# Moving the first transfers, one strip's weight stream and the start of attention in a hand-ordered attention and MLP kernel

## The chip, the cores and the metric

The kernel runs on one core of a Trainium2 chip. The metric is the device time of one execution in microseconds (us); the median of several runs stands for the kernel. All data are fp32, apart from the raw weights, which arrive as fp64 and are converted by the kernel.

## The reference

```python
def _attn_ref(q, k, v, g_norm):                    # (8, 8, 576, 64) each
    kv = np.einsum('bhsd,bhse->bhde', k, v)
    out = np.einsum('bhsd,bhde->bhse', q, kv)
    rms = np.sqrt(np.mean(out * out, axis=-1, keepdims=True) + 1e-06)
    return (out / rms * g_norm).astype(np.float32)

def _moe_ref(x, w_in, w_out):                      # 4608 tokens, 512 -> 2048 -> 512
    h = x @ w_in
    r = np.maximum(h, 0.0)
    g = r * r
    return (g @ w_out).astype(np.float32)

# x is the attention's output, transposed to (batch * seq, heads * dim)
```

Linear attention without a softmax: each head's 64 x 64 matrix kv is built first, and each query row is multiplied by it, divided by its root mean square and scaled. The result feeds a two-layer MLP with a squared relu.

## The kernel before

**Strips.** The 4608 tokens are worked on in nine strips of 512, numbered 0 to 8 in the program. In a strip, "up" is the product with w_in and the squared relu, "down" is the product with w_out and the output. Both use Strassen's scheme: seven products of sums of blocks in place of eight products of blocks. Strip 0 has a plain up (`first_up`, `up_first`) and a down of seven products, in the order 1, 2, 5, 6, 7, 3, 4, each in two halves (`down`, L729 in `product`). Strip 1 has an up of seven products and a down in which the scheme is used twice (`down_deep`, L944). Strips 2 to 8 use it twice in both; their up consists of 55 slots (`up_slot`, L1132 the matmuls, L1144 the sums behind them). The sums of blocks are elementwise work: of weights, of x, of the activations (tiles gt, g_s) and of results (snap, o_sb). Most of it runs on VectorE (DVE), through the helper `minus` (L287) and others; some on GpSimd (POOL). ScalarE (ACT) evacuates results and does the squared relus.

**Attention.** Heads go in pairs p of 0 to 3. `transposed_query` (T) transposes q (on TensorE, L399, for the first batches), `key_value` (K, L427) builds kv, `first_queries` (Q, L541) or `query` multiplies, and the mean of squares (L480), root and reciprocal with Newton steps (L481 to L495, one of them on ACT at L486) lead to x_n (L548 in strip 0, L531 later). x_n is transposed again on TensorE (xt_ps, L565 and L591) or written to memory and read back (x_q, x_d) in late strips. `first_normalized` (N) and `first_features` (F) are these steps of the first strip. All these steps are entries of one list, `slices`, in the order in which they are to be issued; `attend(n)` issues them up to entry n, and the loop over a strip's steps calls it between matmul steps.

**The weights at the start.** The raw w_in and w_out come in pieces of 512 KB (`load_piece`, L237). A piece is first read by ACT (`convert_on_act`, L249 and L252) and then converted by four DVE instructions (`conversion`, L261, L263, L267, L270); `first_piece` issues a number of these steps, so that (piece, (0, 4)) is all four of piece 0. `load_more` keeps loads ahead. `first_up` (U, L576) uses the converted pieces. `keep_busy(ps, n)` (L371) issues n matmuls with the identity whose result is not used.

**The weight stream.** `stream(n)` issues the loads of the next n blocks of w_out (or of sums of w_in) into tiles w_blk of the pool `stream_pool`, which has four buffers of 1 MB (L824 for the blocks of strip 0). The same pool gives `reserve(p)` its tile w_t: for the second use of the scheme, sums of the weight block of product p are made on DVE (`deep_sums`, L287) and stored to memory (`store_deep_sums`, L857; product 6 has its own small tiles, L851). `down` puts product p in `deep_due` at its first half (product 1 at its second), and the loop over strip 0's steps takes it from there. A tile of a pool waits for its buffer's last use: of a w_blk that is the last matmul with it, of a w_t the landing of its store. `store_first(b)` stores three block combinations that were made in SBUF.

**Order and queues.** The program sets the order of every engine's instructions by hand (`manual_schedule`). Each engine runs its instructions in that order, and an instruction waits for its inputs and for its buffers. Nearly all loads and stores are issued on SyncE's queue (SP) in program order; each carries one of eight semaphores in turn.

In strip 0 the steps are numbered i; the first `n_up` are the up part. What follows a step of the down part there:

```python
            if i == n_up:
                stream()
            if i == n_up + 3:
                store_first(2)
...
            while deep_due and i != n_up + 1:
                store_deep_sums(*deep_due.popleft())
```

Of the kernel before, what the change touches and what calls it, by code (L numbers as in the profile page):

```python
# [10 lines left out]
FP32 = mybir.dt.float32  # L11
# [9 lines left out]
def kernel(  # L21
# [34 lines left out]
    nc = tc.nc  # L56
    P = 128
# [4 lines left out]
    NP = H // 2  # L62
    FC = d_ff // P
    C = S // P
# [33 lines left out]
    ctx.enter_context(tc.manual_schedule())  # L98


    main = {}

    def load(b, p, q_eng, names="kvq", parts=range(4)):
        hs = slice(2 * p, 2 * p + 2)
        inputs = (("q", q, q_eng), ("k", k, nc.sync), ("v", v, nc.sync))
        if b == 0 and p >= 2:

            h_place = g_pool.tile([P, 4, C * P], FP32, name="first_qkv", tag="gt")
        if b == 1 and p == 2:
            h_place = spare_pool.tile([P, 3, C * P], FP32, name="more_qkv")  # L110
        placed = (b, p) in ((0, 2), (0, 3), (1, 2))
        for i, (n, src, eng) in enumerate(inputs if b == 0 else inputs[1:] + inputs[:1]):
            if n not in names:
                continue
            whole = src[b, hs, 0 : C * P].rearrange("h (sp c) d -> sp h c d", c=C)
            if n == "q" and b >= Q_ON_PE:

                t = qkv_pool.tile([P, 4 * C, SQ], FP32, name=n, tag=n, bufs=3) if 0 in parts else main[n, b, p]
                for a in parts:
                    h, f = divmod(a * SQ, D)  # L120
                    eng.dma_start(
                        out=t[ts(a, SQ)],
                        in_=src[b, 2 * p + h, 0 : C * P, f : f + SQ].rearrange("(k i) f -> i k f", k=4 * C),
                    )
            elif n != "q":
                if placed:
                    t = h_place[:, i].rearrange("p (h c d) -> p h c d", h=2, c=C)
                else:
                    t = qkv_pool.tile([P, 2, C, D], FP32, name=n, tag=n)
                eng.dma_start(out=t, in_=whole)  # L130
            elif b == 0:

                if placed:
                    t = h_place[:, i].rearrange("p (h c d) -> p h c d", h=2, c=C)
                else:
                    t = qkv_pool.tile([P, 2, C, D], FP32, name=n, tag=n, bufs=3)
                eng.dma_start(out=t, in_=whole)
            else:

                if placed:  # L140
                    t = h_place[:, i].rearrange("p (c h d) -> p c h d", h=2, c=C)
                else:
                    t = qkv_pool.tile([P, C, 2, D], FP32, name=n, tag=n, bufs=3)
                for h in range(2):
                    eng.dma_start(out=t[:, :, h, :], in_=whole[:, h])
            main[n, b, p] = t
# [34 lines left out]
    def load_next(q_eng=nc.sync, names="kvq"):  # L181
        u = next(to_load, None)
        if u is not None:
            load(*u, q_eng, names)
# [49 lines left out]
    def load_piece():  # L234
        if len(raw) < len(sources):
            t = raw_pool.tile([P, 2, WN // 2], I64, name="raw", tag="raw")
            nc.sync.dma_start(out=t, in_=sources[len(raw)])  # L237
            raw.append(t)
# [42 lines left out]
    def load_more(end):  # L281

        while len(raw) < min(end + 8, max(len(sources) - 4, end + 4), len(sources)):
            load_piece()
# [60 lines left out]

    load_next()
    load_rest(0, nc.sync)
    for p in range(1, NP):
        load_next()
        load_piece()  # L350
    load_more(0)
    g_col = const.tile([P, 1], FP32, name="g_col")
    g_src = g_norm.rearrange("(d u) -> d u", u=1)
# [13 lines left out]
    def keep_busy(ps, n):  # L367


        for _ in range(n):  # L370
            nc.tensor.matmul(ps, lhsT=ident, rhs=ident[:, : ps.shape[1]], start=True, stop=True)  # L371
# [38 lines left out]
    def key_value(b, *ps_of):  # L410
        while any(f == load and a[:2] == (b, p) or f == load_rest and a[0] == b for _, f, a in keys_due for p in ps_of):
            _, f, a = keys_due.popleft()
            f(*a)
        ps = apsum.tile([P, len(ps_of), D], FP32, name="kv_ps", tag="at")
        if (b, ps_of[0]) == (0, 0):
            keep_busy(ps[:, 0], 5)
            warm = apsum.tile([P, NT, P], FP32, name="x_ps", tag="first")[:, 0]
        half = slice(REST * (b % 2), REST * (b % 2 + 1))
        tiles = [[main.pop((n, b, p)) for n in "kv"] for p in ps_of]
        steps = [(i, c) for i in range(len(ps_of)) for c in range(C)] + [(i, C) for i in range(len(ps_of))]  # L420
        for i, c in steps:
            if (b, ps_of[i], c) == (0, 0, C):
                keep_busy(warm, 2)
            for h in range(2):
                at = (slice(None), h, c) if c < C else (half, 2 * ps_of[i] + h)
                a, w = (t[at] for t in (tiles[i] if c < C else (k_rest, v_rest)))
                nc.tensor.matmul(  # L427
                    ps[ts(h, D), i], lhsT=a, rhs=w, start=i == 0 and c == 0, stop=c == C, skip_group_check=True
                )
        at = (NP * b + ps_of[0]) % (2 * NP)  # L430
        d = kv_all[:, at : at + len(ps_of)]
        nc.scalar.copy(d[0:D, :, 0:D], ps[0:D])
        nc.scalar.copy(d[D:P, :, D:P], ps[D:P])
        for i, p in enumerate(ps_of):
            kvd[b, p] = d[:, i]
            if b < 2:
                if b == 1 and p == 0:
                    load_next()
            else:
                u = next(to_load, None)  # L440
                if u is not None:
                    keys_later(load, *u, nc.sync, "kv")
                if p == NP - 1 and b + 1 < B:
                    keys_later(load_rest, b + 1, nc.sync)
# [192 lines left out]
        convert_on_act, transposed_query, key_value, first_queries, first_normalized, first_features, first_piece  # L637
    )
    U = first_up
    slices += [(T, (0, 0)), (K, (0, 0)), (T, (0, 1)), (Q, (0,)), (K, (0, 1)), (N, (0,)), (act, (0,)), (piece, (0, 4))]  # L640
    slices += [(T, (0, 2)), (Q, (1,)), (F, (0,)), (K, (0, 2)), (N, (1,)), (act, (1,)), (U, (0, [0])), (piece, (1, 4))]
    slices += [(T, (0, 3)), (Q, (2,)), (F, (1,)), (U, (0, [1])), (K, (0, 3)), (N, (2,)), (act, (2,))]
    slices += [(Q, (3,)), (U, (0, [2])), (F, (2,)), (U, (1, [0])), (piece, (2, 1)), (N, (3,)), (act, (3,))]
    slices += [(piece, (2, 3)), (U, (1, [1, 2])), (F, (3,)), (piece, (3, 4))]
    slices += [(U, (2, [0, 1, 2])), (U, (3, [0, 1, 2]))]
    ready[0] = len(slices)
# [212 lines left out]
    def down(s, p, i):  # L859
        if i == 0:  # L860
            open_bank(p)
        a = {1: 11, 2: 21, 6: 11, 7: 12, 3: 21, 4: 22}.get(p)
        w = w_blk[s, p]
        product(
            p, i,
            lambda fc: (gq[s, 1, fc // 2][:, fc % 2] if p == 5 else gq[s, a][:, fc])[:, ts(i, P)],
            lambda fc: w[:, :, fc], FQ,
        )

        if i == (p == 1) and s == DEEP - 1:  # L870
            deep_due.append((p, w))
        if i == 0:
            return
        del w_blk[s, p]

        if s == 0 and p in (2, 6, 3):
            reserve({2: 5, 6: 7, 3: 4}[p])
        if p not in (1, 7) and (s, p) not in ((0, 3), (0, 4)):
            stream()
        if p == (1 if s else 2):  # L880
            for g in range(NG):
                x = gq[s, 11][:, ts(g, 2)]
                minus(nc.vector, x, gq[s, 1, g], x)
        if p == (2 if s else 6):
            minus(nc.vector, gq[s, 21], gq[s, 21], gq[s, 11])

        def store(th, eh):
            def f(b, a=None):
                o = out_tile()
                if a is None:  # L890
                    nc.scalar.copy(o, b)
                else:
                    nc.vector.tensor_tensor(out=o, in0=b, in1=a, op=ALU.add)
                send(s, th, eh, o)
            return f

        combine(p, store(0, 0), store(0, 1), store(1, 0), store(1, 1))
# [284 lines left out]
    for s in range(N_STRIP):  # L1182
# [23 lines left out]
        for i, (w, fn, a) in enumerate(steps):  # L1206
# [33 lines left out]
            if s:  # L1240
# [6 lines left out]
                elif not due(keys_due) and not (soon and due(tiles_due)):  # L1247
                    least = 2.1 if s == DEEP else 4.5 if i < n_up else 3.3
                    quiet = n_up * 2 // 3 < i < n_up + 3 or s == DEEP and i > n_up + 5
                    if not quiet and clock[0] >= dripped[0] + least:  # L1250
                        dripped[0] = clock[0]
                        drip(True)
                pace = 25 if s == DEEP else 36
                attend(begun + (goal - begun) * min(i + 1, pace) // pace)
                if s == DEEP and i == n_up - 3:
                    leaf_sums(s, 4)
                if s == 1 and i in range(2, 23, 3):
# [2 lines left out]
                    stream()  # L1260
                continue
            if i == n_up:
                stream()
            if i == n_up + 3:
                store_first(2)
            if i in (n_up + 8, n_up + 11):
# [8 lines left out]
            n = i + 1 - (n_up - 6)  # L1275
            pairs, m = divmod(max(n - 2 * NP, 0), 3)
            attend(min(ready[0] + min(max(n, 0), 2 * NP) + (n >= 2 * NP) + 4 * pairs + (0, 2, 2)[m], goal))
            while deep_due and i != n_up + 1:
                store_deep_sums(*deep_due.popleft())
            if 11 <= i < n_up:  # L1280

# [31 lines left out]
```

## Time and profile before

| what | value |
|---|---|
| median of 3 runs | 898.0 us (897.18 to 898.66) |
| profiled execution | 897.15 us |
| its span, from the first to the last instruction | 895.1 us |
| granted TensorE clock, mean | 1.00 |
| busy: PE (TensorE matmul) | 880.4 us, 98% |
| busy: DVE (VectorE) | 734.5 us, 82% |
| busy: ACT (ScalarE), POOL (GpSimd) | 315.7 us, 307.1 us |
| moved by DMA | 235.71 MB, 263 GB/s |

Busy times are those of a profiled execution on the core; a span of 895.1 us holds 20697 instructions. "PE" is the matmul side of TensorE, "PEld" its weight loads, which overlap; "SPq" is SyncE's queue of DMA issues. L12 is line 12 of the kernel. A group "out<-in" names the tiles that an instruction writes and reads. Two records of an fp32 matmul with a 128x128 block of moving data start about 0.112 us apart, so an extra distance between starts is time in which TensorE waited.

### The profile page before, as it was taken

The numbers are of one execution on the slowest core, as the hardware profiler recorded it, in microseconds if no ns is written. First come the engines' busy times: TensorE is split into PE (matmuls) and PEld (weight loads), VectorE is DVE, ScalarE is ACT, GpSimd is POOL, SyncE is SP. The second block draws the span as 40 slices with busy tenths as digits, with TensorE's granted clock in tenths as the row PEclk, the third lists the DMA queues.
The fourth block names the chain that finished last, engine by engine and source line by source line (L and its number), as shares of the span: only waits on it lengthen the run. The fifth ranks groups of instructions, "written<-read, shape, count | busy, mean of one in ns | idle before, by whom it ended". The sixth has DMA issues, their size and how long they took to land.

```text
span 895.1 us, 20697 instructions
## 1 busy us (share of the span) xinstructions
PE 880.4 (98%) x8300; PEld 823.0 (92%) x8300; DVE 734.5 (82%) x1256; ACT 315.7 (35%) x622; POOL 307.1 (34%) x315
## 2 busy tenths in 40 slices
PE   8999999999999999999999999999999999999998
PEld 7445878889999999999999999999999999999998
DVE  3999999779779986898689966895899779875886
ACT  4798241320027302640255023801271027102710
POOL 0000005700558233632373035604460447044700
PEclk9999999999999999999999999999999999999999
DMA  9998998999988798969877989798748865884384
GB/s 303 307 316 250 310 330 267 289 314 323 313 197 279 266 326 238 277 249 317 250 232 238 323 239 248 237 297 292 218 143 297 304 203 164 301 299 154 128 316 180
DMA packets 169231, 235.71 MB, mean 263 GB/s; under 512 B 79408, under 2 KB 134192, under 8 KB 160688
## 3 DMA queue, kind: packets, MB, share of 16 engines
q1 hardware_dynamic: 168976, 234.40, 81.2%
q8 instruction: 65, 1.06, 0.5%
q14 instruction: 30, 0.25, 0.1%
q10 hardware_dynamic: 160, 0.00, 0.0%
HBM read 197.66 MB, written 36.70 MB: 262 GB/s over the span
## 4 chain that ended last, share of the span: by engine, by line
PE 74%; DVE 13%; DMA 6%; issue 2%; ACT 2%; SPq 2%; DVEq 0%; ACTq 0%
PE ps_B L944 22%; PE ps_A L944 17%; PE ps_A L1132 15%; PE ps_B L1132 8%; PE ps_A L729 4%; PE ps_C L1132 3%; PE ps_B L729 2%; PE kv_ps L427 1%; DVE w_c L267 1%; PE x_ps L463 1%; DVE gt L1144 1%; DMA w_blk<-w_in_deep 1%; DVE w_t L287 1%; DMA v_rest<-in_v_dram 1%; DMA x_d<-x_q 1%
## 5 line engine op out<-in xcount | busy, mean ns | idle before, releaser
L944 PE MATMUL ps_B<-w_blk,g_s 128*128 128x128 f32 x1024 | 126.2, 275 | 0.0
L944 PEld LDWEIGHTS ps_B<-w_blk,g_s 128*128 128x128 f32 x1024 | 120.0, 192 | 0.2
L1132 PE MATMUL ps_A<-x_l,w_in 128*128 128x128 f32 x784 | 104.1, 276 | 0.0
L287 POOL TENSOR_TENSOR x_l<-xT 128x256 f32<-128x256 f32 x21 | 16.2, 769 | 246.4 <-PE ps_A L944 246.4
L944 PE MATMUL ps_B<-w_blk,gt 128*128 128x128 f32 x768 | 97.4, 275 | 0.0
L1132 PEld LDWEIGHTS ps_A<-x_l,w_in 128*128 128x128 f32 x784 | 95.4, 192 | 0.5 <-DVE gt L1144 0.2
L944 PE MATMUL ps_A<-w_blk,g_s 128*128 128x128 f32 x768 | 93.6, 275 | 0.0
L944 PEld LDWEIGHTS ps_B<-w_blk,gt 128*128 128x128 f32 x768 | 91.5, 192 | 0.1
L944 PEld LDWEIGHTS ps_A<-w_blk,g_s 128*128 128x128 f32 x768 | 89.6, 192 | 0.0
L1144 POOL TENSOR_TENSOR snap<-snap,gt 128x512 f32<-128x512 f32 x35 | 46.6, 1332 | 118.9 <-ACT snap L1149 54.7
L1149 ACT COPY snap<-ps_A 128x512 f32<-128x512 f32 x63 | 36.7, 583 | 133.5 <-PE ps_A L1132 119.5
L1082 ACT ACTIVATE gt<-gt 128x512 f32<-128x512 f32 x112 | 69.6, 622 | 18.1 <-DVE gt L1144 18.0
L959 DVE TENSOR_TENSOR o_sb<-o_sb,ps_B 128x256 f32<-128x256 f32 (+1 forms) x128 | 49.5, 387 | 30.9 <-ACT o_sb L960 19.2
L944 PE MATMUL ps_A<-w_blk,gt 128*128 128x128 f32 x576 | 72.3, 275 | 0.0
L1083 ACT ACTIVATE gt<-gt 128x512 f32<-128x512 f32 x112 | 70.6, 631 | 3.6
L944 PEld LDWEIGHTS ps_A<-w_blk,gt 128*128 128x128 f32 x576 | 68.2, 192 | 0.4 <-DMA w_blk<-w_deep 0.2
L1144 POOL TENSOR_TENSOR gt<-gt,snap 128x512 f32<-128x512 f32 x42 | 52.6, 1278 | 23.8 <-DVE snap L1144 23.7
L287 DVE TENSOR_TENSOR gt<-gt 128x2048 f32<-128x2048 f32 (+1 forms) x29 | 59.7, 2063 | 0.0
L1042 POOL TENSOR_TENSOR w_i<-w_in 128x512 f32<-128x512 f32 x7 | 9.7, 1382 | 142.2 <-DVE w_in L287 141.5
L960 ACT COPY o_sb<-ps_A 128x128 f32<-128x128 f32 x24 | 6.4, 266 | 146.2 <-PE ps_A L944 146.2
L1132 PE MATMUL ps_A<-x_l,w_blk 128*128 128x128 f32 x392 | 52.2, 276 | 1.3 <-issue 1.2
L1132 PE MATMUL ps_B<-x_l,w_blk 128*128 128x128 f32 x392 | 52.0, 276 | 0.0
(180 smaller groups left out, 1811.7 us busy)
## 6 DMA issues: line engine op xcount, KB each, us to landing
w_blk<-w_deep SPq DMA_DIRECT2D x56, 1024.0 KB, 6.8
w_blk<-w_out SPq DMA_DIRECT2D x56, 768.0 KB, 6.0
w_blk<-w_in_deep SPq DMA_DIRECT2D x49, 768.0 KB, 4.8
raw<-in_moe_w_in_dram SPq DMA_DIRECT2D x16, 512.0 KB, 7.4
raw<-in_moe_w_out_dram SPq DMA_DIRECT2D x16, 512.0 KB, 6.2
k<-in_k_dram SPq DMA_DIRECT2D x29, 256.0 KB, 4.8
v<-in_v_dram SPq DMA_DIRECT2D x29, 256.0 KB, 5.0
x_d<-x_q SPq DMA_DIRECT2D x27, 256.0 KB, 5.3
```

What stands on the lines that cost most here:

```text
L267: yield nc.vector.scalar_tensor_tensor(out=ci, in0=high, scalar=-(2**30), in1=ci, op0=ALU.bitwise_and, op1=ALU.bitwise_or)
L287: eng.tensor_tensor(out=out, in0=a, in1=b, op=ALU.subtract)
L427: nc.tensor.matmul(ps[ts(h, D), i], lhsT=a, rhs=w, start=i == 0 and c == 0, stop=c == C, skip_group_check=True)
L729: nc.tensor.matmul(bank[BANK[p]][:, i, :], lhsT=lhsT(k), rhs=rhs(k), start=p in (1, 5, 2) and i == 0 and k == 0, stop=k == n - 1, skip_gro ...
L944: nc.tensor.matmul(chain[c][x][:, i, :], lhsT=a[:, f, :], rhs=w[:, f, :], start=x not in opened[c] and f == 0, stop=f == FQ // 2 - 1, skip ...
L959: add = lambda out, a, b: nc.vector.tensor_tensor(out=out, in0=a, in1=b, op=ALU.add)
L1042: nc.gpsimd.tensor_tensor(out=s1, in0=w_half(b, 0, 1), in1=w_half(b, 1, 1), op=ALU.add)
L1082: nc.scalar.activation(o, o, AF.Relu)
L1083: nc.scalar.activation(o, o, AF.Square)
L1132: nc.tensor.matmul(ps[:, i, :], lhsT=w, rhs=rhs, start=j in (1, 2, 5) and i == 0, stop=True, skip_group_check=True)
L1144: add = lambda eng, out, a, b: eng.tensor_tensor(out=out, in0=a, in1=b, op=ALU.add)
L1149: nc.scalar.copy(t, ps)
```

## The change

Four places change.

- **First loads.** For pairs 2 and 3 of batch 0, q is loaded ahead of a raw piece, and k and v behind it; before, a raw piece followed each pair's q, k and v. `first_places` keeps the tile of such a pair between the two calls of `load`.
- **First warm-up and first slices.** `keep_busy` ahead of the first `key_value` issues 3 matmuls instead of 5. In the list of the opening's steps, the fourth conversion step of pieces 0 and 1 is taken apart from the first three and comes later, the first U moves behind T of pair 3, and U with index 2 of tile 0 moves ahead of the last Q.
- **Strip 0's down part.** Two blocks (6 and 7) are streamed at its first step instead of one; the loads at the end of products 5 and 6 go, and one (block 4) is issued after the first half of product 6. The sums of product 5's weights, which were made after its first half, are made after its second.
- **Attention of strips 2 and on.** The slices of the next strip are spread over steps 5 to 40 of a strip in place of 0 to 35. For strip 1 nothing changes there.

```diff
-    main = {}
+    main, first_places = {}, {}
...
         if b == 0 and p >= 2:
-
-            h_place = g_pool.tile([P, 4, C * P], FP32, name="first_qkv", tag="gt")
+            if p not in first_places:
+                first_places[p] = g_pool.tile([P, 4, C * P], FP32, name="first_qkv", tag="gt")
+            h_place = first_places[p]
...
     load_next()
     load_rest(0, nc.sync)
-    for p in range(1, NP):
-        load_next()
+    load_next()
+    for p in range(2, NP):
+        load(0, p, nc.sync, "q")
         load_piece()
+        load(0, p, nc.sync, "kv")
+        next(to_load)
     load_more(0)
...
-            keep_busy(ps[:, 0], 5)
+            keep_busy(ps[:, 0], 3)
...
-    slices += [(T, (0, 0)), (K, (0, 0)), (T, (0, 1)), (Q, (0,)), (K, (0, 1)), (N, (0,)), (act, (0,)), (piece, (0, 4))]
-    slices += [(T, (0, 2)), (Q, (1,)), (F, (0,)), (K, (0, 2)), (N, (1,)), (act, (1,)), (U, (0, [0])), (piece, (1, 4))]
-    slices += [(T, (0, 3)), (Q, (2,)), (F, (1,)), (U, (0, [1])), (K, (0, 3)), (N, (2,)), (act, (2,))]
-    slices += [(Q, (3,)), (U, (0, [2])), (F, (2,)), (U, (1, [0])), (piece, (2, 1)), (N, (3,)), (act, (3,))]
+    slices += [(T, (0, 0)), (K, (0, 0)), (T, (0, 1)), (Q, (0,)), (K, (0, 1)), (N, (0,)), (act, (0,)), (piece, (0, 3))]
+    slices += [(T, (0, 2)), (Q, (1,)), (F, (0,)), (K, (0, 2)), (piece, (0, 1)), (N, (1,)), (act, (1,)), (piece, (1, 3))]
+    slices += [(T, (0, 3)), (U, (0, [0])), (Q, (2,)), (F, (1,)), (U, (0, [1])), (K, (0, 3)), (piece, (1, 1)), (N, (2,))]
+    slices += [(act, (2,)), (U, (0, [2])), (Q, (3,)), (F, (2,)), (U, (1, [0])), (piece, (2, 1)), (N, (3,)), (act, (3,))]
...
-        if p not in (1, 7) and (s, p) not in ((0, 3), (0, 4)):
+        if p not in (1, 7) and (s, p) not in ((0, 5), (0, 6), (0, 3), (0, 4)):
             stream()
...
-                pace = 25 if s == DEEP else 36
-                attend(begun + (goal - begun) * min(i + 1, pace) // pace)
+                begin, pace = (0, 25) if s == DEEP else (5, 36)
+                attend(begun + (goal - begun) * min(max(i + 1 - begin, 0), pace) // pace)
...
             if i == n_up:
-                stream()
+                stream(2)
...
+            if i == n_up + 6:
+                stream()
-            while deep_due and i != n_up + 1:
+            while deep_due and i not in (n_up + 1, n_up + 4):
                 store_deep_sums(*deep_due.popleft())
```

## The prediction

> **What bounds the kernel now.** Times are of the profiled execution: 897.15 us, a span of 895.1 and 2.05 around it. I read the busy shares and the slices first, then busy time by stretches of 25 us, then TensorE's waits, last the timeline at each wait. Strips are numbered 0 to 8 as in the program, so "strip three" of the change is strip 2.
>
> ```profile
> PE 880.4 (98%) x8300; PEld 823.0 (92%) x8300; DVE 734.5 (82%) x1256; ACT 315.7 (35%) x622; POOL 307.1 (34%) x315
> ...
> PE   8999999999999999999999999999999999999998
> ...
> DVE  3999999779779986898689966895899779875886
> ```
>
> TensorE is never free for long: what can be won is its idle time. The 82% of VectorE (DVE) hides that it is full in slices 2 to 7. The stretches show where (columns: stretch, its length, busy of PE, PEld, DVE, ACT, POOL, clock, DMA share, GB/s):
>
> ```profile
> 0.00:25.00 25.00, 21.55 (x217) 17.64 (x218) 10.45 (x30) 12.48 (x29) 1.60 (x7) 1.00 0.93 313
> 25.00:50.00 25.00, 23.91 (x62) 10.57 (x61) 23.73 (x53) 20.63 (x41) 0.00 (x0) 1.00 1.06 292
> 50.00:75.00 25.00, 25.00 (x83) 11.54 (x82) 25.00 (x54) 24.41 (x53) 0.00 (x0) 1.00 0.85 283
> ...
> 100.00:125.00 25.00, 24.04 (x177) 20.68 (x176) 24.06 (x45) 10.57 (x14) 0.00 (x0) 1.00 0.91 314
> 125.00:150.00 25.00, 23.98 (x172) 20.34 (x172) 24.59 (x35) 4.83 (x8) 5.41 (x4) 1.00 0.89 279
> ```
>
> From 12.47 us, where DVE starts, to 158.7, where strip 1's last x_n (L531) leaves it, DVE has some 3.5 us of holes in 146. In this front TensorE and DVE are both full; later only TensorE is. TensorE's waits (us in total, times, longest):
>
> ```profile
> PE ps_A L576 <- DVE w_in L270: 1.8, 2, 1.1
> PE ps_B L1132 <- DVE snap L1144: 1.7, 3, 0.7
> ...
> PE xt_ps L591 <- DVE x_n L531: 1.3, 2, 1.0
> PE ps_A L1132 <- issue: 1.2, 1, 1.2
> PE ps_B L729 <- DVE w_in L287: 1.0, 1, 1.0
> PE t_ps L399 <- DMA first_qkv<-in_q_dram: 0.8, 1, 0.8
> PE x_ps L541 <- ACT kv_all L433: 0.5, 1, 0.5
> ```
>
> Placed by the timeline, as start-to-start distance beyond the 0.112 us of a 128x128 record: 12.47 us +0.98 (q of pair 2), 16.75 +0.96 and 29.20 +1.23 (w_in pieces 0 and 2), 22.91 +0.71; then 117.66 +1.13 and 158.13 +0.51 (x_n), 126.76 +1.19; from strip 2 on 6.2 in fifteen places, the largest 1.39 at 531.6. In all 14 us. One label misleads: at 126.76 the profile names DVE, but the weight block of product 3 was issued at 117.72 and landed at 128.03, and TensorE went on at 128.16. That is a DMA wait.
>
> **What the Trainium skill says.** "TensorE: Matmul & The Clock Gate", Part 1: the array falls to half clock after an idle window of about 3.4 us. No stall above is longer than 1.4 us and the granted clock is 1.00 throughout, so none costs clock. The same page (Architectural detail) calls VectorE strictly first in, first out. The trace agrees: at 531.6 TensorE needs the sum snap (L1144), which starts only at 532.37, behind an o_sb sum and a qT transpose of attention. "DMA: Bandwidth & Descriptors" (Anatomy of one DMA) says that a semaphore wait is held by the issuing sequencer; so one SP issue that waits for a buffer holds everything behind it. The trace has it: the load of product 3's block waits for product 2's stored sums (DVE done 108.77, store landed 113.61) and stands fourth behind other stores.
>
> **The change, part by part.**
>
> **Opening.** Fewer warm-up matmuls: the ten 128x64 records (L371, kv_ps) start from 6.5 to 7.9 us; four go, about 0.11 to 0.14 each, 0.45. Their inputs are ready (v landed at 6.12), so everything behind starts 0.45 earlier: DVE at 12.0. Transfers: q of pair 2 is issued one 512 KB piece and q of pair 3 one piece and a k, v pair earlier. Landings in this queue follow each other by 0.66 us per 256 KB and 1.7 per 512 KB, so q2 lands at about 10.6 instead of 13.34, piece 0 at 12.5 instead of 11.87; k2 and v2 hardly move. That removes the 0.98. Piece 0 still comes before DVE needs its words. Order: a conversion's last step (L270, 0.61 us) now follows the next Q and F, so it fills DVE's hole in the root mean square's trip over ACT (0.27, 0.28, 0.44, 0.26 us) and the square is not queued behind it. Followed by hand through the queues (T 1.02, Q 1.09, K 0.86, F 0.47, U 0.86; a piece 2.4 of DVE: 0.46+0.46+0.83+0.61), the end of the opening comes 1.0 earlier on both engines: 0.45 from the warm-up, 0.55 from holes. Bounds 0.4 (the holes open elsewhere) and 1.3 (all holes closed). From 48 to 54 us ACT starts each raw piece 0.08 us after it lands, with the queue full; the pieces do not come earlier, so TensorE is held to its old time there: it has 0.33, 0.31 and 0.73 us of slack at 56.4, 59.8 and 63.7 behind ACT's copies (L777), and keeps perhaps 0.3. DVE is 1.5 us clear of these landings and keeps 1.0.
>
> **Strip 0's down products.** The four block loads stay four. Block 7 goes with 6 at about 102.4 instead of 109.15, block 3 at the end of product 2 into a buffer of stored sums (store landing 110 to 116), so it lands by about 121 where TensorE wants it at 126: the 1.19 goes. The sums for product 5 (four of 0.65 us, 112.89 to 115.5) move behind the x_n of strip 1's tile, which is then ready near 116: the 1.13 at 117.66 goes. So TensorE is 2.3 + 0.3 = 2.6 earlier at 128. But the x_n at 158.7 waits for DVE's own work, none of which is removed: DVE brings 1.0, plus the holes of 0.28 (117.18) and 0.1 of 0.48 (153.44). TensorE, 2.6 early, then waits there for an x_n 1.4 early. Net for the front **-1.4**, between 0 and -2.6.
> Price: block 4 is now issued in the middle of product 6, before 6's buffer is free, so it takes product 5's sums' buffer and waits for that store to land. Issued near 118, 3.8 (unloaded row) to 8.3 us (the 115.53 store) makes 122 to 126; with SP held, little is queued before it, so 4.8 us (102.42 to 107.21) give 127 to 131; product 4 starts at about 132.5. I count 0. Behind it on SP stand product 6's four stores and the k, v and q loads of batches 1 and 2; v_rest landed at 148.32 and is used at 149.23. A block of 3 us or more there would be felt.
>
> **Strips 2 and on.** Attention is spread over slots 5 to 40 of 55 instead of 0 to 35: same instructions, later. Its loads follow its own slots and its stores have a strip's time; the SP row shows room (weight loads wait for TensorE's release of a buffer). So only DVE's queue matters. Removed: stalls at slots 10 to 17, where the last strip's output sums and attention now meet less: 1.39 and 0.17 in strip 5, 0.19 and 0.21 in strip 4, 0.16 in strip 2, and a few under 0.1, **-2.2**. Added: attention's last 2 to 3 us of DVE per strip come at slots 36 to 40, and from slot 42 on the leaf sums fill DVE without it. A tally of DVE work by slot against 0.9 us of TensorE per slot puts the queue there up by 1.0 to 1.9 in strips 2 to 6; less the attention matmuls that move along, about half of it stays. Strip 2 stalled 0.56 at 293.0 with the longest such queue (4.7 us), so I take 0.9 more there and 0.7 in strip 5, nothing in the others: **+1.6**. No trace shows this order, so both ends: all removed and nothing new, the 559 to 565 stalls (1.4) gone too, -3.6; a stall of 1.2 in each of five strips, +3.8. Net **-0.6**.
>
> Sum: -1.4 - 0.6 = -2.0; 895.15 by the profiled execution, and since that one lay 0.85 below the median of the runs, **896.0**.
>
> **The rivals.**
> (A, 0.55) As summed: 893 to 896.2.
> (B, 0.22) The pinned stages take the front's gain down to its DVE holes (-0.5), and the slots cancel (-2.2 + 2.2): 897.5. For: ACT's pinned starts, DVE full up to 158.7. Against: the two removed stalls are real DMA and order waits.
> (C, 0.15) DVE's queue decides at the end of each up phase: slots 42 to 54 are already tight (slack behind DVE 0.5 to 0.98 us there in strips 3, 4, 6, 8). If the whole tallied backlog of 1 to 1.9 us counts in five strips, +6 - 2.2 - 1.4 = +2.4, **900.4**. It is slower from the point where each strip loses over 0.7 us net.
> (D, 0.08) SP stands still for product 5's store: with landing at 129 and a full queue behind (10.3 us, the 117.72 row) block 4 lands at 136 to 139, product 4 waits 4 to 6 us, and later loads move too: 2.6 - 5 = +2.4 in the front, 899.8. Decides when block 4 lands after 134.
>
> **Numbers.** A measurement of this kernel tells about 0.2% (1.8 us) from no change: below 896.2 is faster, above 899.8 slower. B and the upper part of A make "same", with the lower edge of D: faster 0.53, same 0.27, slower 0.20. The range leaves out the best tenth of A (-5 and beyond) and half of the slower cases: 893.0 to 900.0.
>
> **What would show it.** Right: no wait for first_qkv near 12.5; DVE's first reduction at 12.0; the end of the opening 1 us earlier; no wait at L591 near 116 and at L729 near 125; instead a longer wait at strip 1's L591 near 157. Slots 10 to 17 free of waits, a few new ones for snap or gt (L1144) at slots 42 to 54. The L824 row shows block 4's issue waiting for the L857 store. Wrong: TensorE already 2 us early at 70 us or the L591 wait near 157 gone (then the front gives 2.6); product 4 waiting for w_blk; or over 1 us of L1144 waits in a strip's late slots.

## The result and the profile after

The changed kernel takes 903.9 us (median of 9 runs, 901.4 to 906.37) against 898.66 (9 runs, 897.18 to 901.18): ratio 1.0056, 95% interval 1.0043 to 1.0068, slower by 5.0 us (3.9 to 6.1). The forecast was 896.0, between 893 and 900. The profiled execution took 903.43 us with a span of 901.3, that is 6.2 us more than the profiled one before; the latter lay 1.5 us below the median of its nine runs, so the two traces stand further apart than the medians.

TensorE's busy time is 882.3 us, 98% of the span as before. The waits have moved (the five largest below the start-up, in us: total, times, longest; lines are four higher than before):

```profile
PE ps_B L1136 <- DVE snap L1148: 2.2, 4, 0.8
PE ps_A L1136 <- DVE snap L1148: 2.0, 2, 1.5
PE kv_ps L431 <- DMA v_rest<-in_v_dram: 1.9, 1, 1.9
PE kv_ps L431 <- DMA v<-in_v_dram: 1.9, 1, 1.9
...
PE ps_A L733 <- DVE o_sb L897: 1.2, 1, 1.2
```

The waits for x_n at 117 and for a weight block at 126 are gone. In their place stand two waits for attention's transfers (v and v_rest of batch 2), one for a result sum on DVE (o_sb), and more waits for snap. Where the time goes is seen from the starts of the same instruction in both traces (changed minus before, us; the column heads are times in the trace before):

| | 60 | 110 | 122 | 130 | 140 | 152 | 170 | 236 | 890 |
|---|---|---|---|---|---|---|---|---|---|
| TensorE | -0.2 | -0.1 | -1.4 | -2.65 | -1.2 | +5.1 | +5.0 | +5.0 | +6.2 |
| DVE | -0.3 | -0.3 | 0.0 | +1.2 | +1.2 | +1.2 | +5.0 | | |

Up to 130 us TensorE does what was forecast: 2.65 early. Between 130 and 152 it loses 7.8. The timeline has the two waits at their place, first in the changed kernel, then, without a wait, in the kernel before:

```profile
149.49 0.72 PE L431 MATMUL kv_ps<-v,k 128*64 128x64 f32 x16 [1.85 <-DMA v<-in_v_dram]
152.11 0.37 PE L431 MATMUL kv_ps<-v_rest,k_rest 64*64 64x64 f32 x2 [1.90 <-DMA v_rest<-in_v_dram]
...
148.15 1.15 PE L427 MATMUL kv_ps<-v,k 128*64 128x64 f32 x32
149.23 0.45 PE L427 MATMUL kv_ps<-v_rest,k_rest 64*64 64x64 f32 x8
```

and the busy times by stretches show what came with them (changed kernel; columns as in the forecast; the clock stands behind POOL):

```profile
145.00:150.00 5.00, 3.15 (x48) 2.52 (x40) 4.96 (x4) 1.18 (x2) 4.69 (x3) 1.00 0.81 179
150.00:152.50 2.50, 0.60 (x15) 0.46 (x10) 2.46 (x4) 0.00 (x0) 1.90 (x2) 0.50 0.53 107
152.50:156.50 4.00, 4.00 (x15) 3.16 (x13) 1.57 (x3) 0.52 (x2) 3.84 (x4) 0.50 0.65 238
156.50:160.00 3.50, 3.50 (x17) 3.05 (x16) 1.40 (x2) 0.69 (x2) 3.37 (x3) 0.95 1.02 272
```

From 150.0 to 156.8 us TensorE's clock is granted at half. Behind the second wait eight records start 0.21 us later than usual; with the smaller delays before and after them 2.3 us are lost that no list of waits shows. The 7.8 are so made up: 1.35 near 132, 2.04 and 2.12 at the two waits (start to start), and 2.3. In all nine runs of the changed kernel the mean clock was 0.996 to 0.998. (The kernel before loses clock too, but not in every run: of its 139 runs beside the experiments below 48 have a mean clock of 0.998 or less, and their median is 899.9 us against 897.9 of the others.)

Why v came late begins in the issues on SP (issue and landing, us):

| transfer | before | changed |
|---|---|---|
| block 7 (1 MB) | 109.15, 116.24 | 103.42, 111.89 |
| stored sums of product 1 (1 MB) | 106.25, 110.07 | 105.92, 114.42 |
| stored sums of product 2 (1 MB) | 108.79, 113.61 | 108.46, 116.84 |
| block 3 | 117.72, 128.03 | 114.49, 122.70 |
| store_first(2), second half | 113.95, 120.08 | 115.84, 126.58 |
| stored sums of product 5 | 115.53, 123.84 | 119.51, 128.93 |
| block 4 | 123.71, 133.99 | 123.51, 133.26 |
| last of product 6's four stores | 123.08, 130.63 | 126.55, 135.94 |
| v of batch 2, pair 1 | 140.18, 144.71 | 141.72, 149.36 |
| v_rest of batch 2 | 144.50, 148.32 | 148.81, 151.97 |

Block 7's megabyte, which is wanted only at 119, now stands ahead of the stores of product 1's and 2's sums. They land 3 to 4 us later; block 3 waits on SP until 114.49 for one of their buffers, with store_first(2) behind it; and DVE, which may overwrite w_in only when store_first(2) has landed, stops (the second line is the kernel before, where the same three sums run through):

```profile
126.71 1.30 DVE L288 TENSOR_TENSOR w_in<-w_in 128x512 f32<-128x512 f32 x2 [1.16 <-DMA w_out<-w_in]
...
124.82 2.02 DVE L287 TENSOR_TENSOR w_in<-w_in 128x512 f32<-128x512 f32 x3
```

That is the 1.2 us by which DVE is late from 126 on. It comes back to SP: the last store of sums ahead of these loads needs DVE and is issued at 139.00 instead of 137.85. So v is issued 1.5 us later than before, but it lands 4.7 later, because it is under way for 7.6 us instead of 4.5. In e5 below, with the same order of issues, v was under way for 5.1 us (140.06 to 145.13); so a part of the lateness changes from one execution to the next, and what lengthens the transfer is not shown.

From strip 2 on, the wait at slot 10 of strip 5 (1.39) is gone, and others have come at slots 38 and 39, where attention now ends. In strip 5:

```profile
569.56 1.29 DVE L535 TENSOR_TENSOR x_n<-x_ps,newton 128x512 f32<-128x512 f32 x2
570.76 0.68 DVE L1148 TENSOR_TENSOR snap<-ps_A,gt 128x512 f32<-128x512 f32 x1
...
571.50 0.71 PE L1136 MATMUL ps_A<-x_l,w_blk 128*128 128x128 f32 x4 [1.55 <-DVE snap L1148]
```

It is the same collision as before (a snap sum queued behind x_n), at another place. Added up as start-to-start distances beyond the usual, over strips 2 to 8: slots 38 and 39 rise from 1.20 to 5.65, all other places fall from 4.27 to 1.50 (0.74 of block and v waits before left aside).

### The profile page after: what moved, and what is told of

Read it like the earlier page. It is cut to its first block, busy times and chain, and to the rows that moved or that the text cites. A ratio compares the mean times of both kernels' runs of the same rounds, so it can differ in the third digit from the quotient of the medians.

```text
span 901.3 us, 20692 instructions
## 1 busy us (share of the span) xinstructions
PE 882.3 (98%) x8296; PEld 824.3 (91%) x8296; DVE 730.1 (81%) x1256; ACT 316.5 (35%) x622; POOL 307.3 (34%) x315
## 3 DMA queue, kind: packets, MB, share of 16 engines
q8 instruction: 65, 1.06, 0.5%
## 4 chain that ended last, share of the span: by engine, by line
PE 77%; DVE 13%; DMA 5%; issue 2%; SPq 1%; ACT 1%; DVEq 0%; ACTq 0%
PE ps_B L948 22%; PE ps_A L1136 17%; PE ps_A L948 17%; PE ps_B L1136 9%; PE ps_C L1136 4%; PE ps_A L733 2%; PE kv_ps L431 2%; DVE w_c L268 2%; PE ps_B L733 2%; PE x_ps L467 1%; DMA raw<-in_moe_w_in_dram 1%; DMA w_out<-w_in 1%; DVE w_t L288 1%; DVE wt L288 1%; DVE gt L1148 1%
```

## The experiments

Each ran beside the kernel before on the same chip; the ratio is to that kernel.

| run | what differs | ratio, 95% interval | us |
|---|---|---|---|
| e1_opening | opening alone | 0.9997 (0.9986 to 1.0008) | 898.4 |
| e2_down | strip 0's down part alone | 1.0034 (1.0019 to 1.0050) | 902.2 |
| e3_shift | five slots' shift alone | 1.0023 (1.0011 to 1.0035) | 901.2 |
| e4_hold | hold-back of product 5's sums alone | 1.0004 (0.9993 to 1.0014) | 899.0 |
| e5_filler | changed, idle matmuls in the two waits | 1.0041 (1.0024 to 1.0058) | 902.3 |
| e6_first | changed, store_first(2) earlier | 1.0055 (1.0036 to 1.0074) | 903.2 |
| e7_late4 | changed, block 4 as before | 1.0040 (1.0019 to 1.0061) | 902.6 |
| e8_both | both repairs, no shift | 1.0023 (1.0014 to 1.0033) | 900.5 |
| e9_loads | opening, hold-back, batch 2's loads earlier | 1.0002 (0.9988 to 1.0015) | 898.0 |
| e10_after_loads | changed, batch 2's loads earlier | 1.0044 (1.0026 to 1.0061) | 902.4 |
| e11_5to35 | attention over slots 5 to 35 | 1.0028 (1.0012 to 1.0043) | 901.5 |
| e12_0to40 | attention over slots 0 to 40 | 1.0018 (1.0007 to 1.0029) | 899.7 |
| e13_extra | before, 1 MB more of DMA | 1.0041 (1.0025 to 1.0057) | 902.1 |
| e14_parts | changed, product 6's stores later | 1.0052 (1.0034 to 1.0071) | 902.9 |
| e15_hold_parts | e9_loads, product 6's stores later | 1.0001 (0.9989 to 1.0013) | 898.3 |

**The parts one by one.** e1 has the edits of `load`, the first loads, `keep_busy` and `slices`; e2 those around `stream` and `deep_due`; e3 only `begin, pace`.

> Only the opening's part of the change: order of the first transfers, 3 warm-up matmuls instead of 5, order of the first slices. Theory (the loss of 5 us comes from late k, v loads of batch 2 behind strip 0's rearranged stores): the opening keeps about 0.3 us at 36 us and 0.1 at 115 as in the changed kernel, so the median lies within 0.5 us of the kernel before, no wait for v or v_rest near 148. Rival (the opening's transfers, of which raw piece 0 landed at 14.59 instead of 11.87, push the whole SP queue back and with it the loads at 148): 2 to 5 us slower, with waits for v at 147 to 151. In both, piece 0 lands late again if its order in the queue is the cause, and near 12.5 if it was an accident of one execution.

> Only strip 0's down part: block 7 streamed with 6, block 4 in the middle of product 6, product 5's weight sums after its second half. Theory: +3 to +5 us by itself: no waits at 117 and 126 (-2.3), then a wait of 1.2 for DVE near 132, two waits of about 2 us for v and v_rest at 147 to 151, and the granted clock at half for some 3.5 us behind them. Rival (opening and down part are bad only together): within 1 us of the kernel before, the loads landing by 149.

> Only the five slots' shift of attention in strips 2 to 8. Theory: +1.2 us, as between 240 us and the end of the two profiles (5.04 late to 6.21 late): the wait of 1.4 at slot 11 of strip 5 goes, new waits for snap (L1144) of 0.6 to 1.7 come at slots 41 to 46 of strips 2 to 6. Rival (the forecast's sum, and the loss in the two profiles is the noise of one execution): -0.6 us. Rival 2 (the changed kernel enters strip 2 with other queues): no difference.

The ratios less 1 add up to 0.0054, against 0.0056 of the whole change: within the intervals the parts act by themselves. The opening does nothing measurable, the down part costs 3.1 us, the shift 2.1. The theories of e1 and e2 held; the shift cost more than the 1.2 expected, which still lies inside its interval (1.0 to 3.1). These sizes are taken from the ratios because single traces spread: at 236 us e3, e11 and e12, whose program up to there is that of the kernel before, stand 1.8 to 2.7 us later than the trace before, e3 and e11 with waits for weight blocks. Some 2 of the 5.0 us by which the changed kernel is late at 236 are therefore probably the luck of the one trace before. In e1, raw piece 0 landed at 14.02, q of pair 2 at 10.89: the late piece belongs to the order. DVE was 0.9 us early from 50 to 130 us, TensorE 0.7 at 110, and then:

```profile
PE ps_B L733 <- DMA w_blk<-w_out: 1.9, 1, 1.9
PE xt_ps L595 <- DVE x_n L535: 1.4, 2, 0.8
```

Block 3 lands at 127.97, as before at 128.03, so what TensorE is early it waits longer, and after that wait the clock fell to half for 3.4 us (0.57 over 128 to 132). The gain was spent on a longer wait, and the clock took more.

**The hold-back alone.**

```diff
-            while deep_due and i != n_up + 1:
+            while deep_due and i not in (n_up + 1, n_up + 4):
```

> Only the hold-back of product 5's weight sums by one half product (deep_due), all streams as before. Theory: the wait at 117.66 (1.1 us) goes, since x_n is no longer queued behind the sums; the wait for block 3 at 126.8 remains, perhaps longer, since the stores of product 5's and 6's sums are issued later on SP; the k and v loads of batch 2 come at most 1 us later. Sum -0.5 to +1 us. Rival (the hold-back is what delays the loads: the sums' store blocked SP from 119.5 to 123.5 in the changed kernel): +2 to +4 us with waits for v at 147 to 151.

No difference: the waits at 117 and 126 are both gone (between 110 and 130 us TensorE gains 2.5, with DVE unchanged), but v_rest landed at 149.16 and TensorE waited 1.54 for it. So the cost in e2 is that of the streams' new order, of block 7 and block 4 together.

**The clock.** In the loop of `key_value`, seven 128x64 matmuls with the identity stand ahead of each of the two waiting places.

> The changed kernel, with 7 matmuls (128x64, identity, result unused, together about 1.5 us) in front of each of the two places in key_value of batch 2, pairs 0 and 1, at which TensorE waited for v (2.04 us) and v_rest (2.12 us). Theory (two idle stretches of 2 us within 5 us make the clock gate halve the clock: 0.21 us more for each 256-column record from 152.7 to 156.3, about 2 us): the waits shrink to about 0.5 each, the clock stays at 1.00 and the kernel gains 1.5 to 2 us on the changed one, 902 instead of 903.9, though the data land no earlier. Rival (the slow records are not the clock's, or it falls for another reason): the slow records stay and the time is that of the changed kernel or up to 0.5 longer.

In all seven runs the clock was 0.999 or 1.000, and by the ratios the kernel lies 1.4 us below the changed one; the intervals overlap, so the gain itself is only likely, while the effect on the clock is plain. Even with the full clock the kernel stays 3.7 us above the kernel before, so most of the loss is not the clock's. In the execution that was profiled the loads happened to land by 149.3 and no wait is left to compare.

**Repairs of the order on SP.**

```diff
-            if i == n_up + 3:
+            if i == n_up + 2:          # e6, e8: store_first(2) ahead of block 3's load
                 store_first(2)
...
-        ... (s, p) not in ((0, 5), (0, 6), (0, 3), (0, 4)):
+        ... (s, p) not in ((0, 5), (0, 3), (0, 4)):      # e7, e8: block 4 after product 6
```

> The changed kernel, with store_first(2) issued one half product earlier, so that it stands on SP ahead of block 3's load, which waits until 114.4 for the buffer of product 1's stored sums. Theory (that wait holds store_first, whose landing at 126.6 DVE needs for w_in sums, and so all stores and loads behind): the wait of 1.35 near 132 goes, DVE is 1.2 us earlier from 126 on, the loads of batch 2 land about 1 us earlier, the waits at 147 to 152 shrink from 4.2 to at most 2.5 us, and with less than 2 us of idling at once the clock stays up: -2.5 to -4 us against the changed kernel. Rival (the second hold of SP, from 119.5 to 123.5, is what counts): only the 1.35 goes and comes back as a longer wait for v: less than 1 us gained.

> The changed kernel with block 4 streamed at the end of product 6, as in the kernel before, not in its middle; product 5's stored sums and product 6's four small stores then go ahead of it on SP. Theory (block 3's early wait is the cause): product 6's stores are issued from 122 on instead of 123.9, the k and v loads at most 1 us earlier, the wait near 132 stays: 0 to -1.5 us against the changed kernel. Rival (block 4's wait for product 6's buffer holds everything behind it): the k, v, q loads are issued 2 us earlier, the waits at 147 to 152 go below 1.5 us in all and the clock stays: -3 to -4 us.

> The opening's and the down part's change with both repairs (store_first(2) earlier, block 4 at the end of product 6), attention of strips 2 and on as before. Theory: the two removed waits (2.3 us) are kept up to x_n near 158, where DVE's own work ends 0.4 us earlier than before; waits for v at 147 to 150 of at most 1 us: 1 to 2 us faster than the kernel before. Rival (the loads of batch 2 are late in any order that streams block 7 early): no gain, 0 to +2.

The theories of e6 and e8 missed; e7's 1.4 us below the changed kernel (by the ratios) is the upper end of its theory's figure. With store_first(2) ahead, its landing is early (114.83), but the sums' stores, now behind two blocks and it, land at 117.29 and 119.73, and the sums of product 5 wait for that buffer. DVE's waits from 100 to 160 us in e6 (us: total, times, longest):

```profile
DVE w_t L288 <- DMA w_deep<-w_t: 3.5, 1, 3.5
```

In e8 the same wait is 2.2; in e7 it is 0.8, with 0.4 for w_out; in the changed kernel 0.3 and 1.2. In none of the nine traces that leave block 7 at its old place (before, e1, e3, e4, e9, e11, e12, e13, e15) does DVE wait for a store between 100 and 160 us; in all eight that move it ahead of the stores DVE pays, between 0.7 (e10) and 3.5 us (e6), for one buffer or another. No run moves block 7 and nothing else; e8, which issues store_first(2) earlier as well, comes nearest, and it costs 2.1 us where e1, e4 and e9 cost nothing.

For block 4, e7 is less clear. Product 6's stores were issued 1.1 us earlier there and the first k no earlier (127.07 in both), but the second v landed at 145.62 and v_rest at 149.41, and TensorE waited 0.4 us for them in place of two times 2. In exchange it waited 1.4 for block 4 itself (landed 134.78, TensorE on at 134.91). The clock was 1.000 in four of e7's nine runs, against none of the changed kernel's. The 3 to 4 us of the rival did not come, and what block 4's place costs is not separated from no difference.

**Batch 2's loads earlier.**

```diff
-            if i in (n_up + 8, n_up + 11):
+            if i in (n_up + 8, n_up + 9):
                 load_next()
+            if i == n_up + 9:
+                load_rest(2, nc.sync)
```

> The opening's part and the hold-back of product 5's sums alone (streams as before, attention as before), with the second load of k, v, q of batch 2 and load_rest(2) issued two to three half products earlier, ahead of product 7's stored sums on SP. Theory (DVE sets the end of strip 1's up part; its order and buffers are undisturbed here, so its 0.9 us of the opening last to x_n near 158; the loads for 148 to 150 no longer hang on DVE's stores): no waits for v or v_rest, DVE 0.9 earlier at 155, TensorE about 1 us earlier behind it, 897.5 where the kernel before has 898.7, clock 0.999 or more. Rival (the loads only squeeze block 4 or the stores): a new wait for block 4 near 134 or for stores, no gain.

> The changed kernel with the same earlier loads of batch 2. Theory (the waits at 147 to 152 and the half clock behind them are what makes its front 5 us late; behind them stands DVE, 1.2 us late from 126 on by the weight store): both waits go, the clock stays at 0.999 or more, TensorE then waits for x_n about 1 to 1.5 us late near 160: 3 to 4 us better than the changed kernel, 900 to 901. Rival (DVE's lateness alone would cost as much, the loads only come on top of it): less than 1.5 us gained.

In e10 both waits went and TensorE was 1.8 us early at 157, but by the ratios the kernel lies only 1.1 us below the changed one: the rival's figure. In e9, DVE kept its 0.9 and TensorE was 2.1 early at 157, with e15 the best front of all, and it was only 0.2 early at 170 and 1.4 late at 236. The waits of TensorE from 100 to 175 us in e9:

```profile
PE kv_ps L431 <- DMA v<-in_v_dram: 0.8, 1, 0.8
PE ps_A L733 <- DMA w_blk<-w_out: 0.6, 1, 0.6
PE x_ps L467 <- DVE qT L383: 0.6, 1, 0.6
```

The wait for v is that of the next pairs, at 161; that for qT is a transpose behind q's landing, at 166. The theory named the right waits for 148 and was wrong that DVE was the last limit.

**Room for transfers.** e13 copies 2 x 512 KB from one DRAM tensor to another that nothing reads, after the first half of product 6; e14 and e15 issue product 6's four stores behind `load_q_rest(2)`.

> The kernel before with 1 MB more for the DMA engines: two copies of 512 KB from one DRAM tensor to a scratch one that nothing reads, issued on SP in strip 0's down part after the first half of product 6. Theory (the DMA engines have no room in the first 240 us, share 0.95, so every loss or delay there comes out at the end): all landings behind move by 3 us or more, waits for block 4 and for v at 147 to 152, +3 to +5 us, clock below 0.998. Rival (the queue has holes that take 1 MB; only the order on SP and DVE's buffers decide): within 1 us of the kernel before.

> The changed kernel with product 6's four stores of stored sums (1 MB in all) issued behind batch 2's loads, after load_q_rest(2), not at 124 to 127. Theory of room: 1 MB less ahead of the loads of 128 to 149, so k, v and v_rest land 2 to 3 us earlier, both waits and the half clock go, -3 to -4 against the changed kernel, 900 to 901, the rest of the loss being DVE's lateness and the shift. Rival (the loads are late because their issue hangs on DVE's stores at 136 to 140, not on bytes): v is issued and lands as in the changed kernel, less than 1 us gained.

> The opening's part, the hold-back, batch 2's loads earlier, and product 6's stores behind them; streams and attention as before. If the bytes ahead decide, the 0.9 us of DVE from the opening and the earlier loads last past 170: 0.7 to 1.2 us faster than the kernel before. If the DMA work moved behind 150 only meets the loads of the next heads there (as the waits of 1.0 and 0.8 at 161 and 166 did with the earlier loads alone), no gain: within 0.5 us.

One more megabyte, with the order of the other instructions unchanged, costs 3.7 us (2.2 to 5.1). Over the first 240 us the kernel before moves 303 GB/s with a DMA share of 0.95 (last two columns):

```profile
0.00:240.00 240.00, 233.12 (x1688) 181.67 (x1689) 208.62 (x389) 104.20 (x210) 36.92 (x34) 1.00 0.95 303
```

1 MB (1.05 million bytes) at that rate takes 3.5 us. So the front of this kernel has no room left on any of the three: TensorE, DVE and the bytes. That fewer bytes would make it faster no run shows. In e13 the waits are 2.7 us for block 4 and 0.9 for v_rest, with DVE still 1.0 early; the clock, expected below 0.998, stayed at 1.00 in that execution. e14 and e15 remove no bytes, they move them: in e14 v landed at 144.81 and needed no wait, v_rest at 148.61, for which TensorE, 2.3 early, still waited 1.7, and the stores behind pushed the next pairs' v to two waits of 1.0 to 1.2 at 162 to 165, with the clock at half after that. In e14 the loads came earlier as the theory said, and the gain did not come; by the ratios it lies 0.4 us below the changed kernel. e15 gave the second of its two outcomes, no gain, with waits of 1.2 and 0.4 at 161 and 166.

**Where attention lies.** `begin, pace` is (5, 31) in e11 and (0, 41) in e12.

> Only attention of strips 2 and on, begun at slot 5 and ended where it ended before (31 slots' spread, 5 to 35). Theory (the cost of the shift is attention's end at slot 40, next to the sums of slots 41 to 46): the waits for snap at slots 41 to 46 go, the slot 11 wait of strip 5 stays away; within 0.7 us of the kernel before. Rival (the free slots 0 to 4 are lost in any case and the denser work costs the same): +1.5 to +2.5 with waits at slots 12 to 35.

> Only attention of strips 2 and on, begun at slot 0 as before and ended at slot 40 as in the changed kernel (41 slots' spread). Theory (the late end costs): +0.7 to +1.5, with the waits at slots 41 to 46 of strips 2, 3 and 4 as in the changed kernel. Rival (a thinner spread relieves DVE everywhere): 0 to -1.5.

e12 bears out that a late end costs: slots 38 and 39 wait 3.3 us instead of 1.2, in strips 2, 4, 5 and 6, while the wait at slot 10 of strip 5 stays (1.46). In e11 the theory missed and the rival's size came (2.5 us by the ratio), though not at its place. Its largest wait is one of 3.9 us at slot 38 of strip 5, with the clock at half for 3.4 us behind it, and the timeline shows that DVE stood still first, on a transfer:

```profile
564.09 0.71 DVE L379 STREAM_TRANSPOSE qT<-q 128x512 f32<-128x512 f32 x1 [2.24 <-DMA q<-in_q_dram]
...
567.22 1.14 PE L1132 MATMUL ps_B<-xT,w_blk 128*128 128x128 f32 x7 [3.72 <-DVE snap L1144]
```

Squeezed into 31 slots, attention asked for this q before it had landed. All three placements are slower than slots 0 to 35; that the free first slots matter beyond the late end is not separated by these runs.

No kernel tried is shown to be faster than the kernel before; e1, e9 and e15 equal it.

## Why the prediction was wrong

**Opening.** Forecast: both engines 1.0 us early. Shown: DVE 0.3 in the changed kernel's trace, under the lower bound of 0.4, but 0.3 to 1.4 at 50 us in the ten traces with this opening, half of them above 0.95. Six traces with the old opening stand between 1.2 late and 1.0 early, most of them 0.2 to 0.7 early, so about 0.7 is the opening's own. The term that was off is piece 0's landing: 14.6 and, in e1, 14.0, not 12.5, with waits of 0.97 and 0.31 us behind it for the next k and v. (Also, q of pair 3 moves ahead of one piece only, not of a k, v pair as well; it landed at 16.65 instead of 16.93.) That TensorE keeps little of it (0.1 at 110 us here) these traces do not settle: in e3 and e4, with the old opening, it stands 0.9 and 1.2 late there.

**Strip 0's down part.** The two waits of 1.13 and 1.19 went, and TensorE was 2.65 early at 130, against 2.6 forecast. The step that failed is the price: "The four block loads stay four" was taken to mean that their order is free, and block 4 alone was costed ("I count 0"). Block 4 did not wait for the store of product 5's sums (issued at 123.51, that store landed at 128.93), but it was not free either: it landed at 133.26, not by 131, and TensorE had come to product 4 at 132.50. The sum o_sb that product 4 also needs ended at 133.79 and hid it. What above all had to be costed was block 7: its 3.5 us of transfer ahead of the stores that give back buffers. It made DVE 1.2 late where the forecast had it 1.4 early at 158, and v_rest 3.7 late. The text even said "A block of 3 us or more there would be felt": v_rest was issued 4.3 us later. Rival D had this outcome (later loads move too, +2.4) with another trigger and a chance of 0.08; its own trigger, block 4 waiting for product 5's store, did not occur.

**Clock.** The forecast reasoned from the Trainium skill ("TensorE: Matmul & The Clock Gate", Part 1) that no stall of 1.4 us costs clock, and did not ask what clock the new waits would cost. Two waits of 2 us cost 2.3 us more. The reasoning itself held in the profiled execution before (1.00 throughout) but not everywhere: in e14 the clock fell after two waits of 1.2 us, 1.7 us apart, and the kernel before has a lower mean clock in a third of its runs.

**The bound of the front.** The forecast's own stretches carried the missing fact in their last two columns: a DMA share of 0.85 to 1.06 in every stretch shown. TensorE and DVE were followed by hand, the bytes were not. (DVE's idle time from 12.47 to 158.7 us is 5.4 by that stretch's busy time of 140.78, not 3.5.) With the bytes full (e13), time won on an engine is lost again at the next landing, as e1, e4, e9 and e15 each did.

**The shift.** The removed waits were mostly right in kind (2.1 forecast for named places; 2.8 went), the new ones mis-sized and misplaced: 1.6 forecast at slots 42 and on in two strips, 4.5 shown at slots 38 and 39 in five. In place of the net of -0.6 stand +1.7 of waits, and e3 measured +2.1 (1.0 to 3.1). The step that failed is the halving: the tally by slot had the queue up by 1.0 to 1.9 us, and the waits at slots 38 and 39 are 0.6 to 1.9 us in each of strips 2 to 6; to take half of it, and in two strips only, was the error. Rival C was the right one here, at 38 instead of 42. The cost may be larger than this pair of traces has it: against the trace before, the seven traces with attention in slots 5 to 40 lose 0.9 to 5.0 us between 236 and 890 us (median 3.1), the seven with slots 0 to 35 between -1.0 and +1.2 (median -0.7). What the slowest of them lose beyond these slots is not traced.

## What to carry to other kernels

Where an engine stalls in a stretch with the DMA share at 0.95, as here, an earlier transfer is not free: price it by its bytes, and follow what lands later because of it, stores that give back buffers included. When waits move together to one place, ask for the clock as well: here two waits of 2 us cost half as much again. And when work with a queue is shifted, look for the same collision at its new end before counting the old one as saved.

## What was not expected of the hardware

- Waits of about 2 us on TensorE were enough to halve its clock, for 3.4 us (e1, after a wait of 2.0; e8, after 2.5) or 6.8 us (changed kernel, after 2.04 and 2.12; e2). They did not always do it: 2.9 in e13 and 2.1 and 1.9 in e6 left it at 1.00. The same wait of 1.7 us at slot 39 of strip 5 was followed by half clock in e7 (3.4 us from 570.95 on) and not in the changed kernel or e3. So the length of one wait does not decide. The Trainium skill ("TensorE: Matmul & The Clock Gate", Part 1) gives about 3.4 us for the idle window and says that the window runs freely; falls after a single wait of 2 us are below that figure, and here the measurement decides.
- In the ten traces with the new opening the piece of 512 KB that is issued just behind a q transfer landed 1.6 to 4.2 us after it (e15, changed), 3.1 in e1; in the trace before, the same piece, issued ahead of that q, landed 1.9 after the transfer before it.
